# Moving small loads to ScalarE's queue and reordering the first chunk of a decayed attention with mixture-of-experts

## The chip, the cores and the metric

The kernel runs on one core of a Trainium2 chip. The metric is the device time of one execution in microseconds (us). Five engines work side by side on the core: TensorE (PE, matrix products and transposes), VectorE (DVE), ScalarE (ACT), GpSimd (POOL) and SyncE (SP, which here issues transfers between device memory and on-chip memory). Each engine takes its own instructions in order and waits on semaphores for the others. TensorE writes into PSUM, a small memory of a few named tiles, from which VectorE and ScalarE copy on.

## The reference

First a decayed linear attention over 4 sequences, 8 heads, 768 tokens and head size 48, all in float32:

```
state = alpha[t][:, None] * state + k[t] outer v[t]
y[t]  = q[t] @ state
```

Its output, 3072 tokens of 384 numbers, goes into a mixture of 8 experts with one expert chosen for each token:

```
logits = x @ w_gate + modality_bias[modality_id]
e      = argmax(logits);  gate = softmax(logits)[e]
out    = gate * (relu(x @ w1[e]) @ w2[e])
```

The inputs that the change touches are small: `w_gate` (384 x 8), `modality_bias` (2 x 8) and `modality_id` (3072 integers of 8 bytes, 24 KB).

## The kernel before, in words

**Attention.** The 3072 tokens are cut into 24 chunks of 128 tokens, six to a sequence. A loop over steps s = 0 to 23 works on several chunks at once, in the manner of a pipeline: in step s the decay of chunk s is made, chunk s-1 is scaled, scored and added to the state, chunk s-2 gives its outputs, and chunk s-3 goes to memory. For a chunk i:

- `decay_in` (L256) transposes alpha on TensorE (`trans`, L246) and copies it into the tile X, on VectorE for chunk 0 and on ScalarE for all others (L258).
- `decay` (L260) is a scan on VectorE that gives G, the products of the decays from a token to the end of the chunk (L263). `decay_back` (L268) takes a reciprocal and runs a second scan, Fw (L274), the other way.
- `scale` (L287) transposes the keys and multiplies them by G to give kh (L290), then transposes the queries and multiplies them by Fw to give qh (L293).
- `natural` (L296) transposes kh back, `scores` (L304) multiplies kh by qh, `state` (L325) and `outputs` (L335) make the outputs, `update` (L349) adds the chunk to the state.
- `rows` (L364) transposes the outputs of a chunk into rows and SyncE stores them (L374). `logits` and `logits_rows` (L376 to L391) multiply them by the gate weights `wgp`. `guard` (L277) is a check of alpha's range on ScalarE.

The tiles in PSUM that count here: "tr" has three buffers, taken in turn by all transposes of 128 x 512; "sc" has two, for the scores and small products of the routing; "kv" has one, shared by the state update, the logits and, in `bias_table` (L221), the transpose of the modality numbers.

**Loads.** Every chunk has four loads, of alpha, keys, queries and values, each 192 KB in rows of 192 bytes (`load`, L128). Thirteen of them are written ahead of the loop; in step s the loop adds alpha of chunk s+3 and the keys, queries and values of chunk s+2. Alpha, keys and queries have four buffers each, values six.

**The small loads.** `load_gate` (L152) fills `wgp` with four transfers of 3 KB in pieces of 32 bytes, called in step 1; GpSimd clears `wgp` first (L148). `load_modality` (L160) brings in `modality_id` (into `mi`) and `modality_bias` (into `mbb`), called in step 2. `mi` is first read in step 5 by `bias_table`, `wgp` in step 4 by `logits`. All are issued by SyncE.

**The zero matmuls.** `warm(n)` (L142) issues n products of a zero tile into a PSUM tile that nobody reads. Seven stand ahead of the loop, and `trans` adds one behind each of the transposes of chunks 0 and 1 and behind alpha of chunk 2.

**Order.** In the attention loop the instructions of TensorE, VectorE and ScalarE run in the order in which they are written. SyncE and GpSimd are ordered by a planner, which simulates the program with its own costs and may move an issue ahead of another that it takes to be held up. So SyncE's order isn't that of the text: what the profile shows behind the first thirteen loads is alpha 4, keys, queries and values 3, the gate loads, alpha 5, keys, queries and values 4, the modality loads, values 5, two stores of zeros, keys and queries 5, alpha 6.

**Experts.** From about 130 us on, tokens are routed to experts, gathered by index and put through the two layers, each float32 product split into three products of a faster type. TensorE is busy nearly without a break there.

Of the kernel before, what the change touches and what calls it, by code (L numbers as in the profile page):

```python
# [8 lines left out]
F32 = mybir.dt.float32  # L9
# [3 lines left out]
I32 = mybir.dt.int32  # L13
# [8 lines left out]
P = 128  # L22
B, H, S, D = 4, 8, 768, 48
# [5 lines left out]
E = 8  # L29
F = 1024  # L30
NM = 2
N = B * S
NU = N // P
# [29 lines left out]
def attention_moe(ctx: ExitStack, tc: tile.TileContext, q, k, v, alpha, mid, wg, mb, w1, w2, out):  # L63
    nc = tc.nc
    vec, act, pool, pe, sp = nc.vector, nc.scalar, nc.gpsimd, nc.tensor, nc.sync
# [9 lines left out]
    ps = ctx.enter_context(tc.tile_pool(name="ps", bufs=1, space=PSUM))  # L75
# [11 lines left out]
    for i in range(NB):  # L87
        for n, val in (("a", 1.0), ("k", 0.0), ("q", 0.0)):
            t = na.tile([P, H, 64], F32, name=f"nat_{n}{i}")
# [4 lines left out]
    for i in range(NV):  # L94
        t = ac.tile([P, H, 64], F32, name=f"vt{i}")
# [11 lines left out]
    st = {}  # L107
# [20 lines left out]
    def load(i, names="akqv"):  # L128
        b, c = divmod(i, NC)
        for n, t in (("a", alpha), ("k", k), ("q", q), ("v", v)):  # L130
            if n in names:
                dst = VT[i % NV][:, :, :D] if n == "v" else nat[n, i % NB][:, :, :D]
                sp.dma_start(dst, t[b, :, c * P : (c + 1) * P, :].rearrange("h t d -> t h d"))
# [8 lines left out]
    def warm(n):  # L142
        for _ in range(n):
            pe.matmul(idle, still[:, :P], still, start=True, stop=True)

    warm(7)
    wgp = ac.tile([P, 2, 2, 32], F32, name="wgp")
    pool.memset(wgp, 0.0)  # L148
    mi = ac.tile([NU, P, 2], I32, name="mi")
    mbb = ac.tile([P, NM, E], F32, name="mbb")  # L150

    def load_gate():  # L152
        for c in range(2):
            for g in range(2):
                sp.dma_start(
                    wgp[64 * c : 64 * c + D, g, :, :E],
                    wg.rearrange("(h c g d) e -> c g d h e", c=2, g=2, d=D)[c, g],
                )

    def load_modality():  # L160
        sp.dma_start(mi.rearrange("t p w -> t (p w)"), mid.bitcast(I32).rearrange("(t x) -> t x", t=NU))
        sp.dma_start(mbb, mb.unsqueeze(0).broadcast_to([P, NM, E]))


    DR = na.tile([P, SEGS], F32, name="DR")[:, : NP * SEG + 1]
    vec.memset(DR, 0.0)
    vec.memset(DR[:, SEG :: SEG], 1.0)
# [1 line left out]
    for i in range(2):  # L169
        t = na.tile([P, SEGS], F32, name=f"X{i}")[:, : NP * SEG + 1]  # L170
        vec.memset(t[:, 0 :: SEG], 0.0)
        X.append(t)
        t = na.tile([P, SEGS], F32, name=f"DF{i}")[:, : NP * SEG]
        vec.memset(t, 0.0)
        DF.append(t)
    for i in range(3):
        t = ac.tile([P, NP, 64], F32, name=f"T1{i}")
# [43 lines left out]
    def bias_table():  # L221
        mf = ac.tile([NU, P], F32, name="mf")
        vec.tensor_copy(mf, mi[:, :, 0])
        yield
        mp = ps.tile([P, NU], F32, name="kv")
        pe.transpose(mp, mf, ident[:NU, :NU])
        mt = ac.tile([P, NU], F32, name="mt")
        vec.tensor_copy(mt, mp)
        tmp = ac.tile([P, NU, E], F32, name="btt")
        for m in range(NM):  # L230
            sel = ac.tile([P, NU], F32, name=f"msel{m}")
            vec.tensor_scalar(sel, mt, float(m), None, op0=ALU.is_equal)
            vec.tensor_tensor(
                tmp if m else bt,
                sel.unsqueeze(2).broadcast_to([P, NU, E]),
                mbb[:, m].unsqueeze(1).broadcast_to([P, NU, E]),
                op=ALU.mult,
            )
            if m:
                vec.tensor_tensor(bt, bt, tmp, op=ALU.add)  # L240


    def seg(t, lo):
        return t.rearrange("p (a b) -> p a b", b=SEG)[:, :, lo : lo + P]

    def trans(i, n):  # L246
        p = ps.tile([P, NP, P], F32, name="tr", bufs=3)
        for j in range(NP):
            pe.transpose(
                p[:, j], nat[n, i % NB][:, 2 * j : 2 * j + 2].rearrange("p a b -> p (a b)"), ident  # L250
            )
        if i < 2 or (i == 2 and n == "a"):
            warm(1)
        return p

    def decay_in(i):  # L256
        pa = trans(i, "a")
        (act.copy if i else vec.tensor_copy)(seg(X[i % 2][:, 1:], 0), pa)  # L258

    def decay(i):  # L260
        x = X[i % 2]
        G = na.tile([P, SEGS], F32, name="G", bufs=4)[:, : NP * SEG + 1]
        vec.tensor_tensor_scan(  # L263
            G[:, 1:][:, ::-1], x[:, 1:][:, ::-1], DR[:, 1:][:, ::-1], 0.0, op0=ALU.mult, op1=ALU.add
        )
        st[i, "G"] = G

    def decay_back(i):  # L268
        x, d, G = X[i % 2], DF[i % 2], st[i, "G"]
        ac1 = amin[:, i]  # L270
        vec.tensor_scalar(ac1, G[:, 1::SEG], AFLOOR, None, op0=ALU.max)
        vec.reciprocal(d[:, 0::SEG], ac1)
        Fw = na.tile([P, SEGS], F32, name="Fw", bufs=3)[:, : NP * SEG]
        vec.tensor_tensor_scan(Fw, x[:, :-1], d, 0.0, op0=ALU.mult, op1=ALU.add)  # L274
        st[i, "F"] = Fw
# [8 lines left out]
            accum_out=gacc[:, i : i + 1],  # L284
        )

    def scale(i):  # L287
        kh = sb.tile([P, NP, P], F32, name="kh")
        pk = trans(i, "k")
        vec.tensor_tensor(kh, pk, seg(st[i, "G"][:, 1:], 1), op=ALU.mult)  # L290
        qh = sb.tile([P, NP, P], F32, name="qh", bufs=3)
        pq = trans(i, "q")
        vec.tensor_tensor(qh, pq, seg(st[i, "F"], 1), op=ALU.mult)  # L293
        st[i, "k"], st[i, "q"] = kh, qh

    def natural(i):  # L296
        p = ps.tile([P, NP, P], F32, name="tr", bufs=3)
        for j in range(NP):
            pe.transpose(p[:, j], st[i, "k"][:, j], ident)
        kn = na.tile([P, NP, P], F32, name="knat", bufs=2)  # L300
        act.copy(kn, p)
        st[i, "n"] = kn
# [61 lines left out]
    def rows(i):  # L364

        p = ps.tile([P, 2, NP, 64], F32, name="tr", bufs=3)
        for g in range(2):
            for h in range(2):
                pe.transpose(
                    p[:, g, 2 * h : 2 * h + 2].rearrange("p c e -> p (c e)"), st[i, "yt"][:, i % 2, g, h], ident  # L370
                )
        xs = sb.tile([P, DM], F32, name="xs", bufs=4)
        act.copy(xs.rearrange("p (j g d) -> p g j d", g=2, d=D), p[:, :, :, :D])
        sp.dma_start(xd[row(i) : row(i) + P, :], xs)  # L374
# [11 lines left out]
    def logits_rows(i):  # L386
        lp = ps.tile([P, 2, P], F32, name="kv")
        for c in range(2):
            pe.transpose(lp[:, c], st[i, "l"][:, c], ident)
        z = slice(i - 1, i + 1)  # L390
        vec.tensor_reduce(L[:, z], lp.rearrange("p c (j e) -> p c e j", e=32)[:, :, :E], axis=AX.X, op=ALU.add)  # L391
# [409 lines left out]
    def advance():  # L801
        for f in list(flows):
            if next(f, f) is f:
                flows.remove(f)

    def start(f):
        flows.append(f)
        if next(f, f) is f:
            flows.remove(f)
# [5 lines left out]
    def live(i):  # L815
        return 0 <= i < NU

    def groups(i):
        for after, t0, t1 in GROUPS:
            if after == i:  # L820
                start(group_flow(t0, t1))
# [28 lines left out]
    for s in range(NU):  # L850
        if s > 0 and s + PF < NU:
            load(s + PF, "a")
        if s > 0 and s + PF - 1 < NU:
            load(s + PF - 1, "kqv")
        if s == 1:
            load_gate()
        if s == 2:
            load_modality()
        if s == 4:
            sp.dma_start(xd[MID : MID + 1], zr)  # L860
            sp.dma_start(gd[MID : MID + 1], zr[:, 0:1])
        if s != 1:
            decay_in(s)
        if live(s - 1):
            scale(s - 1)
        if s == 1:
            decay_in(s)
        if live(s - 3):
            rows(s - 3)
        if live(s - 4) and s % 2:  # L870
            logits_rows(s - 4)
        advance()
        if live(s - 1) and (s - 1) % NC < NC - 1:
            natural(s - 1)
        decay(s)
        if s < NU - 1:
            advance()
        if s % 2:
            groups(s - 4)
        decay_back(s)  # L880
        guard(s)
        if s == 5:
            start(bias_table())
            half_index()
        if live(s - 3) and (s - 3) % 2:
            logits(s - 3)
        if live(s - 2):
            state(s - 2)
        if live(s - 1):
            scores(s - 1)  # L890
        if live(s - 2):
            outputs(s - 2)
        if live(s - 1):
            update(s - 1)

    L0 = NU - 1
    scale(L0)
    rows(L0 - 2)
    nctx.close()
# [65 lines left out]
    mp = ectx.enter_context(tc.tile_pool(name="mp", bufs=1, reuse_waits="tile"))  # L965
# [163 lines left out]
    for n in range(1, len(seq)):  # L1129
        kind, e = seq[n]  # L1130
# [4 lines left out]
        x, w = n % NX, n % 2  # L1135
# [117 lines left out]
```

## Time and profile before

| | |
|---|---|
| median of 3 runs | 374.81 us (373.77 to 374.91) |
| profiled execution | 375.57 us |
| its span, first to last instruction | 373.6 us |
| TensorE busy | 359.1 us |
| VectorE, ScalarE, GpSimd busy | 224.8, 189.0, 151.6 us |
| attention loop, first to last alpha transpose | 4.2 to 135.8 us |
| transfers | 59.18 MB, mostly in pieces under 512 bytes |

In the rows of a profile the first number is the start in us from the first instruction of the span and the second the duration. Then come the engine (PEld is TensorE's loading of weights, SPq SyncE's queue), the line of the kernel, the operation, output and inputs by tile name, and the shape. In brackets stands how long the engine was idle before, and whose end released it. `xN` says how many instructions of a kind a row merges. For an issue of a transfer the duration is that of the issue, not of the transfer. Rows of stretches give, for a stretch of time, the busy time and number of instructions of PE, PEld, DVE, ACT and POOL, the clock that TensorE was granted (1 is full), the mean load of the 16 DMA engines, and GB/s.

### The profile page before, as it was taken

Reading aid. Unit: us, or ns where it says so; the run is one execution under the profiler, and the core shown is the slowest. Engines: PE = TensorE matmul, PEld = TensorE weight load, DVE = VectorE, ACT = ScalarE, POOL = GpSimd, SP = SyncE. Lnnn points to the kernel's source line nnn. Section 1 sums busy time; section 2 is a strip of 40 time slices with the busy share of each in tenths; the row PEclk is TensorE's granted clock in tenths of the full one; section 3 lists DMA queues with packets and bytes.
Section 4 is the critical chain, followed back from the end, with each engine's and each line's share of the span. In section 5 each row is a group of like instructions: output and inputs, shape, how many; then the busy total and the mean of one; then the engine's idle time right before and its main releaser. Section 6 shows DMA issues by size and latency. Waiting matters only on the chain. (4 is left out here: it accounts for less than half of the span.)

```text
span 373.6 us, 9370 instructions
## 1 busy us (share of the span) xinstructions
PE 359.1 (96%) x3666; PEld 317.0 (85%) x3666; DVE 224.8 (60%) x455; ACT 189.0 (51%) x367; POOL 151.6 (41%) x218
## 2 busy tenths in 40 slices
PE   7998999999999899999999999999999999999992
PEld 4787788889888788799998898899889988978992
DVE  6886979878979977895746506531661455036400
ACT  2666677677678464446554425433551454154310
POOL 9945244534444345283146335412722372220021
PEclk9999999999999989999999999999999999999997
DMA  9989999999999994849756416431723374110011
GB/s 139 165 123 159 208 192 194 183 185 190 198 183 186 194 380 160 294 171 359 223 157 204 155 44 227 154 107 48 270 84 120 131 214 145 45 44 5 1 45 49
DMA packets 122846, 59.18 MB, mean 158 GB/s; under 512 B 102977, under 2 KB 114296, under 8 KB 122792
## 3 DMA queue, kind: packets, MB, share of 16 engines
q1 hardware_dynamic: 118824, 48.83, 58.5%
q0 software_dynamic: 3968, 9.65, 7.7%
q8 instruction: 31, 0.51, 0.6%
q14 instruction: 23, 0.19, 0.2%
HBM read 49.01 MB, written 9.50 MB: 157 GB/s over the span
## 5 line engine op out<-in xcount | busy, mean ns | idle before, releaser
L973 POOL DMA_INDIRECT out_dram<-os,odx x23 | 23.1, 1004 | 110.0 <-ACT os L1041 93.3
L1007 PE MATMUL sc<-w2H,hH 128*128 128x384 f32 x192 | 65.0, 338 | 0.0
L316 POOL TENSOR_SCALAR_AFFINE_SELECT scT<-scT 128x512 f32<-128x512 f32 x48 | 38.4, 822 | 65.3 <-ACT scT L315 65.3
L1009 PE MATMUL sc<-w2H,hL 128*128 128x384 f32 x192 | 64.2, 334 | 0.0
L1008 PE MATMUL sc<-w2L,hH 128*128 128x384 f32 x192 | 64.2, 334 | 0.0
L837 DVE TENSOR_TENSOR w1L<-w1r,w1H 128x768 fp32r<-128x768 f32 x24 | 22.0, 955 | 67.6 <-ACT w1H L835 67.6
L1026 PE MATMUL tr<-xH,w1H 128*128 128x512 f32 (+1 forms) x144 | 53.8, 374 | 0.0
L1028 PE MATMUL tr<-xH,w1L 128*128 128x512 f32 (+1 forms) x144 | 53.5, 372 | 0.0
L1027 PE MATMUL tr<-xL,w1H 128*128 128x512 f32 (+1 forms) x144 | 53.5, 371 | 0.0
L829 DVE SCALAR_TENSOR_TENSOR hL<-tr,hH 128x512 fp32r<-128x512 f32 x47 | 32.4, 689 | 31.5 <-ACT hH L827 31.3
L827 ACT ACTIVATE hH<-tr 128x512 fp32r<-128x512 f32 x47 | 28.1, 598 | 45.5 <-PE tr L1028 42.0
L1041 ACT ACTIVATE os<-sc,gg 128x384 f32<-128x384 f32 x23 | 13.4, 582 | 67.4 <-PE sc L1009 43.5
L1007 PEld LDWEIGHTS sc<-w2H,hH 128*128 128x128 f32 x192 | 36.1, 188 | 1.1 <-issue 1.0
L1008 PEld LDWEIGHTS sc<-w2L,hH 128*128 128x128 f32 x192 | 36.1, 188 | 0.0
L1009 PEld LDWEIGHTS sc<-w2H,hL 128*128 128x128 f32 x192 | 36.0, 188 | 0.0
L699 POOL DMA_INDIRECT gg<-gd,idx x25 | 26.6, 1063 | 21.9 <-DMA gd<-gs 14.9
L315 ACT COPY scT<-sc 128x512 f32<-128x512 f32 x48 | 25.8, 589 | 12.6 <-PE sc L311 12.6
L693 POOL DMA_INDIRECT xg<-xd,idx x25 | 27.0, 1081 | 11.7 <-issue 4.9
L274 DVE TENSOR_TENSOR_SCAN Fw<-X,DF 128x516 f32<-128x516 f32 x24 | 31.0, 1291 | 0.8
L1028 PEld LDWEIGHTS tr<-xH,w1L 128*128 128x128 f32 x144 | 27.1, 188 | 4.7
L1026 PEld LDWEIGHTS tr<-xH,w1H 128*128 128x128 f32 x144 | 27.1, 188 | 4.6
L1027 PEld LDWEIGHTS tr<-xL,w1H 128*128 128x128 f32 x144 | 27.1, 188 | 4.6
(245 smaller groups left out, 684.2 us busy)
## 6 DMA issues: line engine op xcount, KB each, us to landing
w1r<-in_moe_w_dram SPq DMA_DIRECT2D x16, 768.0 KB, 4.8
w2r<-in_moe_w_dram SPq DMA_DIRECT2D x16, 768.0 KB, 4.5
nat_a<-in_alpha_dram SPq DMA_DIRECT2D x24, 192.0 KB, 3.7
nat_k<-in_k_dram SPq DMA_DIRECT2D x24, 192.0 KB, 5.5
nat_q<-in_q_dram SPq DMA_DIRECT2D x24, 192.0 KB, 4.8
vt<-in_v_dram SPq DMA_DIRECT2D x24, 192.0 KB, 4.6
xd<-xs SPq DMA_DIRECT2D x24, 192.0 KB, 4.9
xg<-xd,idx POOLq DMA_INDIRECT x25, 5.4
```

The source lines that it names most:

```text
L274: vec.tensor_tensor_scan(Fw, x[:, :-1], d, 0.0, op0=ALU.mult, op1=ALU.add)
L316: pool.affine_select(s, s, [[0, NP], [1, P]], ALU.is_ge, 0.0, base=0, channel_multiplier=-1)
L693: pool.indirect_dma_start(xg[x][:, u], None, xd[0:rows], IOA(idx[:, c : c + 1], 0), bounds_check=rows - 1, oob_is_err=False)
L699: pool.indirect_dma_start(gg[x][:, u : u + 1], None, gd[0:rows], IOA(idx[:, c : c + 1], 0), bounds_check=rows - 1, oob_is_err=False)
L827: act.activation(hH, hp, AF.Relu)
L829: vec.scalar_tensor_tensor(hL, hp, 0.0, hH.bitcast(F32), op0=ALU.max, op1=ALU.subtract)
L1007: pe.matmul(op, hH[:, us] if f is None else hH[:, f, us], wH, start=first, stop=False)
L1008: pe.matmul(op, hH[:, us] if f is None else hH[:, f, us], wL, start=False, stop=False)
L1009: pe.matmul(op, hL[:, us] if f is None else hL[:, f, us], wH, start=False, stop=final)
L1026: pe.matmul(hp, wH[:, d, fs], XH[:, d, :n], start=(d == 0), stop=False)
L1027: pe.matmul(hp, wH[:, d, fs], XL[:, d, :n], start=False, stop=False)
L1028: pe.matmul(hp, wL[:, d, fs], XH[:, d, :n], start=False, stop=(d == ND - 1))
```

## The change

Five edits. ScalarE issues the four gate loads, ahead of the loop, and the modality and bias loads, at the top of step 3 ahead of that step's alpha copy; SyncE issues none of them any more. `wgp` is cleared on VectorE instead of GpSimd. The transpose of the modality numbers goes into "sc" instead of "kv". A zero matmul stands behind the transposes of chunk 0 and behind alpha of chunk 1 only. For chunk 0 the keys are transposed and scaled in step 0, between the two scans, by a new function `scale_keys`; for all other chunks `scale` calls it, with the same order as before.

```diff
-    pool.memset(wgp, 0.0)
+    vec.memset(wgp, 0.0)
     mi = ac.tile([NU, P, 2], I32, name="mi")
     mbb = ac.tile([P, NM, E], F32, name="mbb")
 
-    def load_gate():
-        for c in range(2):
-            for g in range(2):
-                sp.dma_start(
-                    wgp[64 * c : 64 * c + D, g, :, :E],
-                    wg.rearrange("(h c g d) e -> c g d h e", c=2, g=2, d=D)[c, g],
-                )
-
-    def load_modality():
-        sp.dma_start(mi.rearrange("t p w -> t (p w)"), mid.bitcast(I32).rearrange("(t x) -> t x", t=NU))
-        sp.dma_start(mbb, mb.unsqueeze(0).broadcast_to([P, NM, E]))
-
-
+    for c in range(2):
+        for g in range(2):
+            act.dma_start(
+                wgp[64 * c : 64 * c + D, g, :, :E],
+                wg.rearrange("(h c g d) e -> c g d h e", c=2, g=2, d=D)[c, g],
+            )
...
-        mp = ps.tile([P, NU], F32, name="kv")
+        mp = ps.tile([P, NU], F32, name="sc", bufs=2)
...
-        if i < 2 or (i == 2 and n == "a"):
+        if i == 0 or (i == 1 and n == "a"):
             warm(1)
...
-    def scale(i):
+    def scale_keys(i):
         kh = sb.tile([P, NP, P], F32, name="kh")
         pk = trans(i, "k")
         vec.tensor_tensor(kh, pk, seg(st[i, "G"][:, 1:], 1), op=ALU.mult)
+        st[i, "k"] = kh
+
+    def scale(i):
+        if i:
+            scale_keys(i)
         qh = sb.tile([P, NP, P], F32, name="qh", bufs=3)
         pq = trans(i, "q")
         vec.tensor_tensor(qh, pq, seg(st[i, "F"], 1), op=ALU.mult)
-        st[i, "k"], st[i, "q"] = kh, qh
+        st[i, "q"] = qh
...
-        if s == 1:
-            load_gate()
-        if s == 2:
-            load_modality()
         if s == 4:
             sp.dma_start(xd[MID : MID + 1], zr)
             sp.dma_start(gd[MID : MID + 1], zr[:, 0:1])
+        if s == 3:
+            act.dma_start(mi.rearrange("t p w -> t (p w)"), mid.bitcast(I32).rearrange("(t x) -> t x", t=NU))
+            act.dma_start(mbb, mb.unsqueeze(0).broadcast_to([P, NM, E]))
...
         decay(s)
+        if s == 0:
+            scale_keys(s)
```

## The prediction

> **What bounds the kernel now.** I read the shares of the page first, then the list of who waited for whom on TensorE, then the timeline around the one wait that ends on a transfer, then SyncE's queue ahead of it. Of the page:
>
> ```profile
> PE 359.1 (96%) x3666; PEld 317.0 (85%) x3666; DVE 224.8 (60%) x455; ACT 189.0 (51%) x367; POOL 151.6 (41%) x218
> ```
>
> TensorE is the bound, so what changes the end is TensorE's idle time, or work taken off it. The waits of its matmuls, total, times and longest:
>
> ```profile
> PE tr L249 <- DMA nat_a<-in_alpha_dram: 1.8, 1, 1.8
> ...
> PE kv L381 <- DVE mt L228: 0.4, 1, 0.4
> ```
>
> Both touch the change. The timeline shows them in steps 5 to 7 of the attention loop (start, duration, engine, line; in brackets the idle time ahead and what ended it):
>
> ```profile
> 33.01 1.23 DVE L274 TENSOR_TENSOR_SCAN Fw<-X,DF 128x516 f32<-128x516 f32 x1
> ...
> 33.84 0.62 PE L356 MATMUL kv<-vt,knat 128*64 128x48 f32 x16
> ...
> 34.16 0.59 DVE L223 CAST mf<-mi 24x128 f32<-24x128 int32 x1
> ...
> 35.88 0.17 DVE L523 TENSOR_REDUCE sz<-hz 128x1 f32<-128x13 f32 x1
> 36.24 0.42 PEld L249 LDWEIGHTS tr<-ident,nat_a 128*128 128x128 f32 x4 [1.91 <-DMA nat_a<-in_alpha_dram]
> 36.24 0.66 PE L249 MATMUL tr<-ident,nat_a 128*128 128x128 f32 x4 [1.78 <-DMA nat_a<-in_alpha_dram]
> ...
> 37.38 0.69 DVE L290 TENSOR_TENSOR kh<-tr,G 128x512 f32<-128x512 f32 x1 [1.33 <-PE tr L249]
> ...
> 38.81 0.64 PE L381 MATMUL kv<-yt,wgp 128*32 128x256 f32 x8 [0.41 <-DVE mt L228]
> ...
> 43.33 0.66 DVE L290 TENSOR_TENSOR kh<-tr,G 128x512 f32<-128x512 f32 x1
> ...
> 44.04 0.65 PE L299 MATMUL tr<-ident,kh 128*128 128x128 f32 x4
> ```
>
> TensorE is ready for step 6 at 33.84 + 0.62 = 34.46 and gets alpha chunk 6 only at 36.24: 1.78 us lost. VectorE loses less. Its scan of step 5 and the four small instructions behind it (34.16 to 36.05) run during the wait, and its key scaling at 37.38 is 1.33 late. From there VectorE works on without a gap until the next key scaling ends at 43.99, and TensorE's key transposes at 44.04 start on that. So in these steps VectorE is late next: however early chunk 6 lands, at most 1.33 us come back.
>
> Why is the chunk late? SyncE's issues ahead of it:
>
> ```profile
> 16.87 1.97 SPq L133 DMA_DIRECT2D nat_q<-in_q_dram  x1
> 18.89 1.12 SPq L133 DMA_DIRECT2D vt<-in_v_dram  x1
> 20.11 3.58 SPq L155 DMA_DIRECT2D wgp<-in_moe_w_gate_dram  x4
> 23.79 0.38 SPq L133 DMA_DIRECT2D nat_a<-in_alpha_dram  x1
> ...
> 26.41 1.37 SPq L161 DMA_DIRECT2D mi<-in_moe_modality_id_dram  x1
> 27.82 0.36 SPq L162 DMA_DIRECT2D mbb<-n_moe_modality_bias_dram  x1
> ...
> 28.75 0.39 SPq L860 DMA_DIRECT2D xd<-zr  x1
> ...
> 31.27 1.07 SPq L133 DMA_DIRECT2D nat_a<-in_alpha_dram  x1
> ```
>
> SyncE issues back to back, about 1.1 us a load while the DMA engines are full. Chunk 6 is issued at 31.27 and is there at 36.24, 4.97 later. The four gate loads, 12 KB in all, hold the queue for 3.58 us, and the DMA engines run dry behind them (last two numbers: DMA share, GB/s):
>
> ```profile
> 22.00:23.00 1.00, 1.00 (x27) 0.95 (x24) 0.81 (x1) 1.00 (x3) 0.75 (x1) 1.00 0.24 23
> 23.00:24.00 1.00, 1.00 (x10) 1.00 (x11) 0.00 (x0) 0.80 (x3) 1.00 (x3) 1.00 0.12 9
> ```
>
> **The change part by part.** *SyncE loses six issues.* Behind the v load, which ends at 20.01, stand seven loads, two small stores and then chunk 6. At 1.12 and a gap of 0.06 a load, and 0.45 a store, chunk 6 is issued at 20.06 + 7 × 1.18 + 0.9 = 29.2 and lands at 29.2 + 4.97 = 34.2. VectorE needs the step's key transposes by 36.05, and these end 37.38 − 36.24 = 1.14 after the step starts, so 34.9 is early enough. The margin of 0.7 is less than one issue: if the planner, which orders SyncE anew, puts one more load ahead, about 0.5 of the gain is lost; two cost all of it. Gain: −1.33.
>
> *Zero matmuls.* Three of seven go, all of them in step 2. The rows of the first steps:
>
> ```profile
> 4.12 1.28 ACT L278 ACT_TABLE_LOAD   x1 [4.12 <-DMA nat_a<-in_alpha_dram]
> ...
> 8.45 0.58 ACT L258 COPY X<-tr 128x512 f32<-128x512 f32 x1 [2.32 <-PE tr L249]
> ...
> 9.21 0.67 DVE L290 TENSOR_TENSOR kh<-tr,G 128x512 f32<-128x512 f32 x1
> ...
> 9.80 0.68 DVE L293 TENSOR_TENSOR qh<-tr,Fw 128x512 f32<-128x512 f32 x1
> ...
> 10.03 0.63 PE L299 MATMUL tr<-ident,kh 128*128 128x128 f32 x4 [1.40 <-DVE kh L290]
> 10.39 1.22 DVE L263 TENSOR_TENSOR_SCAN G<-X,DR 128x516 f32<-128x516 f32 x1
> ...
> 10.58 1.10 PE L311 MATMUL sc<-qh,kh 48*64 48x128 f32 x32
> ...
> 12.71 0.38 PE L144 MATMUL y<-still 128*128 128x512 bf16 x1
> ...
> 12.93 0.60 PE L249 MATMUL tr<-ident,nat_k 128*128 128x128 f32 x4
> ...
> 13.57 0.69 DVE L290 TENSOR_TENSOR kh<-tr,G 128x512 f32<-128x512 f32 x1 [0.27 <-PE tr L249]
> ```
>
> Without the zero matmul at 12.71 the key transposes start in its place, 0.22 earlier, and VectorE's scaling at 13.57, idle for 0.27 on them, moves with them: −0.22. The other two stand between transposes that then wait for VectorE anyway: nothing. Could TensorE's clock fall instead? The granted clock (third number from the end) stayed at 1.00 through the idle stretches of 1.40 ahead of 10.03 and 1.78 ahead of 36.24, and the zero matmuls that go stand amid dense work:
>
> ```profile
> 10.00:11.00 1.00, 0.97 (x20) 0.83 (x24) 1.00 (x2) 0.31 (x1) 0.92 (x2) 1.00 1.50 164
> ...
> 36.00:37.00 1.00, 0.76 (x7) 0.76 (x8) 0.05 (x1) 0.06 (x1) 0.41 (x1) 1.00 0.72 121
> ```
>
> No cost, then. The Trainium skill (TensorE: Matmul & The Clock Gate, HAM oscillation) warns that an idle gap of more than about 3.4 us halves the clock; by that rule too nothing happens here, unless gaps add up.
>
> *Keys of chunk 0 ahead of its second scan.* VectorE is busy without a gap over these rows, so the query scaling at 9.80 ends at the same time in either order, and the scores at 10.58 start on it. Only the key transposes at 10.03 come earlier, into TensorE's idle time. Zero; the bound on the gain is that idle time, 1.40, and a cost would need chunk 0's key load later than the scan's end.
>
> *The modality transpose in another PSUM tile.* The 0.41 ahead of 38.81 goes, but VectorE sets 37.38 to 43.99, so it becomes slack: zero (bounds −0.41 and 0). *Clearing the gate tile on VectorE*: it is idle before the first alpha copy; zero.
>
> *Gate loads on ScalarE at the start.* ScalarE waits for chunk 0 until 4.12, and its next copy that others need is at 8.45, idle for 2.32 before: four issues at the 0.36 to 0.9 that such small ones take on SyncE (27.82; 3.58/4) fit. Their packets go beside chunk 0's load, which everything follows. From below 0; from above, 12 KB as four of SyncE's issues, 3.58. The nearest row is 27.82's 0.36 for one small transfer in flight before chunk 0 is complete, shared with it; I take +0.1.
>
> *Modality and bias loads on ScalarE in step 3.* They stand in ScalarE's own order, ahead of the alpha copy (X) of step 3:
>
> ```profile
> 17.62 0.33 ACT L358 COPY S<-kv 128x192 f32<-128x192 f32 x1
> ...
> 18.17 0.59 ACT L258 COPY X<-tr 128x512 f32<-128x512 f32 x1 [0.22 <-PE tr L249]
> ...
> 18.84 0.62 PE L369 MATMUL tr<-ident,yt 128*128 128x128 f32 x4
> ...
> 19.35 0.66 PE L299 MATMUL tr<-ident,kh 128*128 128x128 f32 x4
> ```
>
> Behind the waiting issue stands that copy, and behind the copy stand the output transposes at 18.84: with three buffers named tr they take over the alpha transposes' buffer, and 18.84 is the copy's end, 18.76, and a hop. TensorE has no slack from here to step 6. No row shows an issue on ScalarE. From below: two at 27.82's 0.36 with gaps of 0.05, begun when the copy to S has been dispatched at 17.62, end at 18.44, 0.27 after 18.17; the key transposes at 19.35 can take 0.07 of it: +0.2. (An issue that costs ScalarE nothing: 0.) From above: SyncE's own 1.37 + 0.36 + 0.1 end at 19.45, +1.2. I take +0.2, as SyncE's 1.37 was behind four queued loads and ScalarE's queue is empty then.
>
> **Sum**: −1.33 − 0.22 + 0.1 + 0.2 = −1.25. The profiled execution took 375.57 (span 373.6, 1.97 around it), which gives 374.32; it lies 0.76 above the median of the runs shown, 374.81. On that median the forecast is 373.56, say 373.6. Its own range is 372.9 to 374.6: with the 0.41 ahead of 38.81 and chunk 0 on time, or with SyncE's 1.2 for ScalarE.
>
> **Rivals.** *ScalarE's issues queue behind SyncE's.* While SyncE issues without a pause (16.87 to 23.7), one of its issues takes 1.1 to 1.97. If an issue on ScalarE can only begin where one of SyncE's ends, the two of step 3 cost half a wait (0.57) + 0.36, then a full wait (1.14) + 0.36, with gaps 2.6. Begun 0.22 earlier than 17.62, they end at 20.0, and the X copy is 1.8 late. TensorE stands still ahead of 18.84 for as long. Then −1.33 + 1.8 + 0.1 = +0.6: 375.4, slower than before; with SyncE's longest issue in the way +2.0, 376.8. It decides from about 2 us for the two issues, where the loss equals the gain. For it: SyncE's issue times follow the load on the DMA engines, 0.38 when they are dry and 1.1 when full, so an issue does wait for something shared. Against it: ScalarE has no load of its own outstanding then. The Trainium skill (Perfetto Trace Analysis, DMA Instruction — HWDGE) says that the two issuing sequencers share one descriptor generator, locked for the length of an issue; by that rule this rival holds, and the time is its 375.4. No row here shows two sequencers issuing at once.
>
> *Chunk 6 lands no earlier.* The DMA engines are full, or the planner fills the freed places with loads and stores that were further back. Then −0.22 + 0.3 remain: 374.8. For it: only 0.7 of margin. Against it: the two windows in which the engines are dry, over 2 us of transfer time.
>
> *The gate loads delay chunk 0.* If its load lands with or after the four, everything behind 4.12 shifts by up to 3.58, the stall's end included, since VectorE's chain sets that. It decides at 1.3 us; at 2.5 the sum is −1.33 + 2.5, 376.0. Against it: chunk 0 is issued first and 16 times as large as the four together.
>
> **How the numbers follow.** 0.3% of the time is 1.12 us, about what a measurement of this kernel tells from none. Forecast 0.52 (faster 0.38, same 0.14: its −1.25 is near the bound). Queueing on ScalarE 0.26 (faster 0.02, same 0.15, slower 0.09). Chunk 6 no earlier 0.12 (same 0.11, slower 0.01). Late chunk 0 0.10 (same 0.04, slower 0.06). Together faster 0.40, same 0.44, slower 0.16. TensorE's clock adds spread that the change doesn't steer: it dropped once,
>
> ```profile
> 130.00:135.00 5.00, 5.00 (x80) 3.69 (x79) 4.79 (x20) 2.25 (x6) 2.38 (x3) 0.66 1.03 388
> ```
>
> and a third of the clock for 5 us is 1.7 us, which may be there or not. The range 372.7 to 375.9 leaves out the upper parts of the two slow rivals (0.11) and a run without that drop on top of the full gain (0.07).
>
> **What would show it.** In the changed kernel TensorE should list no wait on an alpha load, and VectorE's first key scaling after its four small instructions should follow them with no idle time; the key transposes of step 7 should wait about 0.9 on VectorE. The X copy of step 3 should start 0.1 to 0.4 after its transposes plus the usual 0.2 idle; 1.5 or more means queueing. ScalarE's four issues at the start should take under 1 us each, and its table load should start at 4.1 to 4.3. Wrong it would be if the wait on chunk 6 stays, if the output transposes of step 3 wait on X for over a microsecond, or if a later wait of the same size takes over.

## The result: 3.1% slower

The changed kernel takes 386.48 us in the median (385.74 to 388.01), the kernel before 374.86 beside it; the ratio is 1.031, with a 95% interval of 1.025 to 1.036. The forecast was 373.6, and the time lies 10.6 us above the upper end of its range. The profiled execution took 386.31, its span is 384.2 against 373.6. The ratios in this document leave out the few executions that ran at a lower clock and more than 1.5% longer than the fastest of their kernel.

The list of waits of the changed kernel has a new head on TensorE and a new entry on ScalarE (total, times, longest):

```profile
PE tr L367 <- ACT X L251: 12.6, 1, 12.6
```

and on ScalarE:

```profile
ACT X L251 <- DMA vt<-in_v_dram: 13.0, 1, 13.0
```

One wait of 12.6 us, once, is longer than the whole loss of 11.6. TensorE waits for ScalarE's alpha copy X, and ScalarE waits for a load of *values*, which its copy doesn't read. The wait on alpha chunk 6, 1.78 before, is gone from TensorE's list. The timeline of the changed kernel around the stall, ScalarE first, then SyncE, then TensorE:

```profile
17.49 0.32 ACT L356 COPY S<-kv 128x192 f32<-128x192 f32 x1
29.12 0.56 ACTq L857 DMA_DIRECT2D mi<-in_moe_modality_id_dram  x1
30.34 0.36 ACTq L858 DMA_DIRECT2D mbb<-n_moe_modality_bias_dram  x1
30.80 0.59 ACT L251 COPY X<-tr 128x512 f32<-128x512 f32 x1 [12.98 <-DMA vt<-in_v_dram]
...
23.86 2.29 SPq L133 DMA_DIRECT2D vt<-in_v_dram  x2
...
28.61 1.07 SPq L133 DMA_DIRECT2D nat_a<-in_alpha_dram  x1
29.77 1.27 SPq L133 DMA_DIRECT2D vt<-in_v_dram  x1
...
17.34 0.66 PE L242 MATMUL tr<-ident,nat_a 128*128 128x128 f32 x4
...
18.27 0.60 PE L242 MATMUL tr<-ident,nat_q 128*128 128x128 f32 x4
31.43 1.12 PE L367 MATMUL tr<-ident,yt 128*128 128x128 f32 x4 [12.56 <-ACT X L251]
...
37.87 0.66 PE L242 MATMUL tr<-ident,nat_a 128*128 128x128 f32 x4
...
43.85 0.66 PE L242 MATMUL tr<-ident,nat_a 128*128 128x128 f32 x4
...
57.68 0.66 PE L297 MATMUL tr<-ident,kh 128*128 128x128 f32 x4 [0.95 <-DVE kh L283]
...
61.22 0.66 PE L242 MATMUL tr<-ident,nat_a 128*128 128x128 f32 x4
...
147.59 0.66 PE L242 MATMUL tr<-ident,nat_a 128*128 128x128 f32 x4
```

The alpha transposes in it (nat_a) begin steps 3, 4, 5, 8 and 23. Those of the kernel before, steps 4, 5, 8 and 23:

```profile
22.89 0.66 PE L249 MATMUL tr<-ident,nat_a 128*128 128x128 f32 x4
...
28.87 0.66 PE L249 MATMUL tr<-ident,nat_a 128*128 128x128 f32 x4
...
47.57 0.66 PE L249 MATMUL tr<-ident,nat_a 128*128 128x128 f32 x4
...
135.50 0.66 PE L249 MATMUL tr<-ident,nat_a 128*128 128x128 f32 x4
```

The issues themselves are short, 0.56 and 0.36, close to the two at 0.36 of the forecast. What it didn't have is the time ahead of them: ScalarE has nothing to do after 17.81 and issues the modality ids only at 29.12.

The stall costs more than its own length. The stretches of the changed kernel (last three numbers: granted clock, DMA share, GB/s):

```profile
22.00:23.00 1.00, 0.00 (x0) 0.00 (x0) 0.00 (x0) 0.00 (x0) 0.00 (x0) 1.00 0.93 174
23.00:24.00 1.00, 0.00 (x0) 0.00 (x0) 0.00 (x0) 0.00 (x0) 0.00 (x0) 0.55 1.00 171
31.00:36.00 5.00, 4.57 (x56) 4.01 (x56) 2.81 (x4) 2.05 (x5) 0.00 (x0) 0.50 1.11 176
130.00:135.00 5.00, 5.00 (x94) 4.18 (x93) 4.84 (x15) 4.21 (x10) 2.03 (x3) 1.00 0.60 130
```

TensorE's clock falls about 4 us after the last matmul (18.87) and is still at half when the work resumes. From the output transposes of step 3 to the next alpha transposes it takes 37.87 − 31.43 = 6.44 us, against 22.89 − 18.84 = 4.05 in the kernel before: 2.39 more. The Trainium skill (TensorE: Matmul & The Clock Gate, HAM oscillation) puts the limit for such a gap at about 3.4 us; for this gap the trace agrees.

The account by the starts of the steps: step 4 begins 14.98 later than before (12.59 of stall and 2.39 of slow clock), step 5 too, step 8 13.65 later. So 1.33 us come back between steps 5 and 8. The drop of the clock between 130 and 135 us (0.66 before) isn't there: the row above has 1.00, and in the trace's clock record it stays at 1.00 from 36.7 to 381.5 us. Step 23 stands at +12.09, 1.56 less than step 8. That is about what the drop costs, half of the 3.4 us from 130.1 to 133.5 in the kernel before. The spans differ by 10.6. What makes the 1.5 us between 12.09 and 10.6, in the experts' part, stays open.

### The profile page after: what moved, and what is told of

It reads as the page before. It is cut to its first block, busy times and chain, and to the rows that moved or that the text cites. A ratio compares the mean times of both kernels' runs of the same rounds, so it can differ in the third digit from the quotient of the medians.

```text
span 384.2 us, 9361 instructions
## 1 busy us (share of the span) xinstructions
PE 358.8 (93%) x3663; PEld 317.4 (83%) x3663; DVE 225.1 (59%) x456; ACT 189.3 (49%) x367; POOL 151.2 (39%) x217
## 5 line engine op out<-in xcount | busy, mean ns | idle before, releaser
L314 POOL TENSOR_SCALAR_AFFINE_SELECT scT<-scT 128x512 f32<-128x512 f32 x48 | 37.6, 807 | 77.5 <-ACT scT L313 77.5
L256 DVE TENSOR_TENSOR_SCAN G<-X,DR 128x516 f32<-128x516 f32 x24 | 29.6, 1232 | 11.7 <-ACT X L251 11.7
L691 POOL DMA_INDIRECT xg<-xd,idx x25 | 27.0, 1079 | 11.6 <-issue 5.2
```

Source lines behind the costliest of these rows:

```text
L256: vec.tensor_tensor_scan(G[:, 1:][:, ::-1], x[:, 1:][:, ::-1], DR[:, 1:][:, ::-1], 0.0, op0=ALU.mult, op1=ALU.add)
L314: pool.affine_select(s, s, [[0, NP], [1, P]], ALU.is_ge, 0.0, base=0, channel_multiplier=-1)
L691: pool.indirect_dma_start(xg[x][:, u], None, xd[0:rows], IOA(idx[:, c : c + 1], 0), bounds_check=rows - 1, oob_is_err=False)
```

## The experiments

**Theory and rivals.** The program as built (a listing of its instructions, no profile) shows what ScalarE waits for. Every transfer of SyncE and ScalarE reports its end on one of eight counters. The counters are handed out in turn, in the order of the planner, and an issue waits until the last transfer on its counter, eight places earlier, is complete:

```
place  engine   transfer       counter  waits for
24     SyncE    values 4       0        place 16
25     SyncE    values 5       1        place 17
26-31  SyncE    zeros, zeros, keys 5, queries 5, alpha 6, values 6
32     ScalarE  modality ids   0        place 24
33     ScalarE  bias           1        place 25
```

In the kernel before, SyncE holds all of these places and comes to them in order, so such a wait looks eight of its own transfers back. ScalarE reaches its two places at 17.8 us, as nothing else holds it; SyncE reaches place 24 at 23.86 and place 25 at 25.00. That is theory A.

The trace of the changed kernel bears the listing out. Its records name the counter (a semaphore) on which each transfer reports and the one for which each issue waits. The modality ids wait for the counter of values 4, whose last report comes at 29.10, and are issued at 29.12. The bias waits for that of values 5, whose last report comes at 30.32, and is issued at 30.34.

The rivals: theory B is the forecast's first rival, ScalarE's issues queueing behind SyncE's for a generator of descriptors; theory C, that another part of the change makes the stall.

**1. The two loads back on SyncE.**

```diff
+        if s == 2:
+            sp.dma_start(mi...); sp.dma_start(mbb...)
-        if s == 3:
-            act.dma_start(mi...); act.dma_start(mbb...)
```

> The change, with only the two loads of step 3 (modality ids, bias) given back to SyncE in step 2. Theory A (each transfer of SyncE and ScalarE takes the next of eight completion counters in the order of the written program, and its issue waits for the transfer eight places earlier; the two loads in step 3 fall behind the transfers of values 4 and 5, which SyncE issues only at 23.9 and 25.0 us): no wait of ScalarE before its copy of step 3, 373.4 us (372.6 to 374.4). Theory B (issues of ScalarE queue behind those of SyncE in one generator): the same here, 373.4, as ScalarE issues nothing in the loop. Theory C (some other part of the change makes the stall, the two loads only stand beside it): the stall of 12.6 us stays, 386.

Measured: 375.85 beside 377.15 for the kernel before on the same chip, ratio 0.996 (0.9941 to 0.9979). No long wait on ScalarE or TensorE. C falls: the other parts of the change together are a gain of 0.4%.

**2. The same two loads, ScalarE, step 1.**

```diff
-        if s == 3:
+        if s == 1:
             act.dma_start(mi...); act.dma_start(mbb...)
```

> The change, with the same two loads issued by ScalarE in step 1 in place of step 3, about 8 us after the start and in the midst of SyncE's first twenty issues. Theory A: eight places earlier stand gate loads 1 and 2, done by 6 us: no wait of ScalarE, 373.3 us (372.5 to 374.4). Theory B: SyncE issues without a gap from 5 to 20 us, so ScalarE's two issues wait for several of its issues of 1.1 us each, or for all of them: 376 to 386 us. Theory C: 386.

Measured: 0.997 (0.9953 to 0.9988). ScalarE's rows of this kernel:

```profile
4.36 0.56 ACTq L857 DMA_DIRECT2D mi<-in_moe_modality_id_dram  x1
5.49 0.36 ACTq L858 DMA_DIRECT2D mbb<-n_moe_modality_bias_dram  x1
```

The issues have the same durations as in the slow kernel, while SyncE issues its first loads beside them. This speaks against B. The expectation put them about 8 us after the start; in fact ScalarE came to them right behind the gate loads. The second was held even here, but briefly: it waits for the second gate load, whose last report comes at 5.47, and is issued at 5.49.

**3. The kernel before with these two loads alone moved to ScalarE's step 3.**

> The kernel before, with only the two loads moved from SyncE's step 2 to ScalarE's step 3; gate loads stay on SyncE. Theory A: the two wait for the transfers of values 4 and 5, which SyncE, behind its gate loads, issues later than in the changed kernel (25.6 and about 27 us in place of 23.9 and 25.0), so ScalarE's copy of step 3 starts at 32 to 33 us in place of 30.8: 386 to 389 us. Theory B: two waits of one issue each, up to 3.6 us: 376 to 378. Theory C: 374 to 375.

Measured: ratio 1.034 (1.031 to 1.037). ScalarE and SyncE in this kernel:

```profile
29.41 0.61 ACTq L861 DMA_DIRECT2D mi<-in_moe_modality_id_dram  x1
30.60 0.36 ACTq L862 DMA_DIRECT2D mbb<-n_moe_modality_bias_dram  x1
31.07 0.59 ACT L258 COPY X<-tr 128x512 f32<-128x512 f32 x1 [13.61 <-DMA vt<-in_v_dram]
...
24.32 2.14 SPq L133 DMA_DIRECT2D vt<-in_v_dram  x2
```

The two loads by themselves make the whole loss. The copy starts at 31.07, earlier than the 32 to 33 expected: the expectation took the issue of values 4 from the kernel before (25.6), but here SyncE spent 2.52 us on the four gate loads, not 3.58, and was there at 24.32.

**4 and 5. ScalarE in step 2, and in step 4.** As in experiment 2, with other steps. If A holds, the wait isn't tied to step 3 but to whatever stands eight places ahead: queries 3 and alpha 5 for step 2, queries 5 and alpha 6 for step 4.

> The change, with the same two loads issued by ScalarE in step 2. Theory A: eight places earlier stand the transfers of queries 3 (issued by SyncE at 18.2 us) and of alpha 5 (at 20.5), which land some 5 us after their issue; ScalarE comes to the loads at about 13 us and is held until about 25: a stall of 11 to 12 us, now in step 2, 384 to 387 us. Theory B: the same place in SyncE's row of issues as step 1 has, so a time as in that run, 376 to 386. Theory C: the stall stays in step 3, 386.

> The change with the two loads issued by ScalarE in step 4 in place of step 3. Theory A (counters): eight places earlier stand the transfers of queries 5 and of alpha chunk 6, issued by SyncE at about 28 to 30 us and there some 5 us later; ScalarE comes to the loads at about 23 and is held until 33 to 35, now ahead of its alpha copy of step 4: TensorE stands still for 10 to 11 us ahead of the output transposes of step 4, its clock falls to 0.5, and the ratio is 1.025 to 1.035. Theory B (the issue queues behind SyncE's open issues for a generator): SyncE's gaps grow from 26 us on, so the wait is shorter than in step 3, under 4 us, ratio 0.997 to 1.008.

Measured: 1.036 (1.0324 to 1.0396) in step 2 and 1.029 (1.0258 to 1.033) in step 4. SyncE's and ScalarE's rows, first of the kernel with step 2:

```profile
18.32 1.00 SPq L133 DMA_DIRECT2D nat_q<-in_q_dram  x1
...
20.24 1.16 SPq L133 DMA_DIRECT2D nat_a<-in_alpha_dram  x1
...
23.10 0.56 ACTq L857 DMA_DIRECT2D mi<-in_moe_modality_id_dram  x1
25.50 0.36 ACTq L858 DMA_DIRECT2D mbb<-n_moe_modality_bias_dram  x1
25.96 0.59 ACT L251 COPY X<-tr 128x512 f32<-128x512 f32 x1 [12.82 <-DMA mi<-in_moe_modality_id_dram]
```

then of the kernel with step 4:

```profile
27.61 0.86 SPq L133 DMA_DIRECT2D nat_q<-in_q_dram  x1
28.56 1.06 SPq L133 DMA_DIRECT2D nat_a<-in_alpha_dram  x1
...
32.69 0.56 ACTq L857 DMA_DIRECT2D mi<-in_moe_modality_id_dram  x1
33.89 0.36 ACTq L858 DMA_DIRECT2D mbb<-n_moe_modality_bias_dram  x1
34.35 0.58 ACT L251 COPY X<-tr 128x512 f32<-128x512 f32 x1 [11.11 <-DMA nat_a<-in_alpha_dram]
```

From the issue of the transfer eight places ahead to ScalarE's issue, in us:

| loads in | first load | second load |
|---|---|---|
| step 2 | queries 3: 23.10 − 18.32 = 4.78 | alpha 5: 25.50 − 20.24 = 5.26 |
| step 3 (the change) | values 4: 29.12 − 23.86 = 5.26 | values 5: 30.34 − 25.00 = 5.34 |
| step 3 (alone) | values 4: 29.41 − 24.32 = 5.09 | values 5: 30.60 − 25.25 = 5.35 |
| step 4 | queries 5: 32.69 − 27.61 = 5.08 | alpha 6: 33.89 − 28.56 = 5.33 |

The issue times 25.00 and 25.25 are those of the second issue in merged rows of two, from the trace's own records. Eight times nearly the same gap, and it is what such a transfer takes from issue to landing in the changed kernel between 14 and 45 us (KB each, median us to landing):

```profile
vt<-in_v_dram SPq DMA_DIRECT2D x7, 192.0 KB, 5.0
...
nat_a<-in_alpha_dram SPq DMA_DIRECT2D x5, 192.0 KB, 5.1
nat_q<-in_q_dram SPq DMA_DIRECT2D x5, 192.0 KB, 5.2
```

This is A, to the transfer. In all eight cases the trace names the counter of the transfer in the table as the one that the issue waits for, and its last report comes 0.02 us before the issue: in step 2 at 23.08 and 25.48, in step 4 at 32.67 and 33.87. No rival is left for the stall. Step 2's ratio, 388 us on the 374.86 of before, is a little above the 384 to 387 us expected and step 4's TensorE wait, 9.6 us, a little under the 10 to 11.

**6. The two loads issued by GpSimd.** In the listing, and in the trace, GpSimd's transfers have counters of their own.

```diff
-            act.dma_start(mi...); act.dma_start(mbb...)
+            pool.dma_start(mi...); pool.dma_start(mbb...)
```

> The change with the two loads of step 3 issued by GpSimd in place of ScalarE. Theory A: in the written program GpSimd's transfers have completion counters of their own, so nothing waits for values 4 and 5 and the stall is gone: ratio 0.995 to 0.998; if GpSimd's issues hold up its first selections (TensorE's step 1 begins after 8.3 us), 0.998 to 1.002. Theory C (the two loads hold up the loop by being in flight in step 3): the stall stays, 1.03.

Measured: 0.9991 (0.9968 to 1.0014), no stall; GpSimd issued the two at 5.41 and 6.16 us without a wait. The engine that issues and the counters change together here, so by itself it doesn't tell A from B; the interval spans both of A's bands.

**7. The gate loads alone on ScalarE.** The kernel before, with `wgp` cleared on VectorE and its four loads issued ahead of the loop by ScalarE.

> The kernel before, with only the four gate loads moved from SyncE to ScalarE ahead of the loop (and the gate tile cleared on VectorE, as this needs). Theory A (the prediction's step 1, with four issues in place of six): SyncE is ahead by 1.0 us or more when it comes to alpha chunk 6, TensorE's wait of 1.78 on it falls to at most 0.3, and VectorE's chain lets 1.3 come back; the gate issues cost 0.05 us at the start: ratio 0.9965 (0.9945 to 0.9985). Theory B (the gain needs the other parts): ratio 1.000.

Measured: 0.9973 (0.9951 to 0.9996). A holds: TensorE no longer waits on alpha chunk 6, and step 8 begins at 46.47, 1.10 earlier than before. As far as these intervals can tell, this part by itself brings all that the change can bring.

**8 and 9. The zero matmuls.** First the kernel before without the three zero matmuls; then the kernel of experiment 2 with all seven again.

> The kernel before, with only the three zero matmuls of step 2 left out. Theory A (the prediction's step 2): step 3 begins 0.1 to 0.2 us earlier, TensorE's clock stays at 1.00 between 10 and 20 us, and the wait on alpha chunk 6 eats the gain: ratio 0.999 to 1.000. Theory B (these matmuls held the clock up): the clock falls to 0.5 for some 3.3 us in step 2, as it did where the two loads stood in step 1 (0.71, 0.50, 0.50, 0.58 from 12 to 16 us), step 3 begins 1.0 to 1.2 later, and the same wait eats that too, down to 0.7: ratio 1.000 to 1.003. The rows of 12 to 18 us tell the two apart, not the time.

> The change with the two loads issued by ScalarE in step 1, as before, and with the seven zero matmuls of the kernel before. Theory B (the zero matmuls hold the clock): the clock stays at 1.00 from 12 to 16 us, step 3 begins at 17.4 to 17.6 us in place of 18.53, and the time falls by up to 1.1 us against that run, to a ratio of 0.994 to 0.996 against the kernel before. Theory A (the drop there had another cause): the drop stays, ratio 0.997 to 0.998.

The reason for asking is in experiment 2's kernel, whose clock fell at the start:

```profile
12.00:13.00 1.00, 1.00 (x18) 0.95 (x15) 0.93 (x3) 1.00 (x3) 1.00 (x5) 0.71 1.41 162
13.00:14.00 1.00, 1.00 (x6) 1.00 (x5) 0.56 (x1) 0.71 (x2) 1.00 (x2) 0.50 1.43 162
...
15.00:16.00 1.00, 0.98 (x5) 0.72 (x4) 0.86 (x2) 0.00 (x0) 0.23 (x1) 0.58 1.46 168
```

and on TensorE's timeline:

```profile
10.69 1.10 PE L309 MATMUL sc<-qh,kh 48*64 48x128 f32 x32 [1.45 <-DVE qh L291]
...
18.53 0.66 PE L242 MATMUL tr<-ident,nat_a 128*128 128x128 f32 x4
```

Its step 3 starts at 18.53, the changed kernel's at 17.34. With the seven zero matmuls (experiment 9) the clock is at 1.00 there and step 3 starts at 17.55. But the time doesn't follow: 0.9971 (0.9952 to 0.9989), as with four. The kernel before without three of them measured 1.0035 (1.0002 to 1.0068). Its profiled execution, 375.25 us, has the clock at 1.00 from 12 to 17 us and step 3 at 17.25, 0.23 earlier than before, as the forecast had it. The mean clock of its executions was 0.991 in the median, against 0.994 for the kernel before. 0.3% of the clock is about the size of the loss; where in those executions it falls isn't shown, and the other kernels with four zero matmuls and no stall have medians of 0.992 to 0.993, where the kernel before has 0.992 to 0.994. So: 0.2 us earlier in the rows, no gain in the time, and a clock that may fall. More isn't settled.

**10. The key scaling alone.**

> The kernel before, with only chunk 0's key scaling moved ahead of its second scan. The prediction's step 3: key transposes of chunk 0 about 1.4 us earlier, its scores within 0.1 of 10.58 us, ratio 0.999 to 1.001. Rival (in the runs with this part the scores began at 10.66 to 10.69 us, in the run with the gate loads alone at 10.16): the key scaling stands in VectorE's row ahead of the second scan and the query scaling ends 0.1 later, which the wait on alpha chunk 6 eats: ratio 1.000 to 1.001 with scores at 10.65 to 10.75.

Measured: 1.0026 (1.0002 to 1.0051). VectorE and TensorE in this kernel:

```profile
8.73 1.23 DVE L274 TENSOR_TENSOR_SCAN Fw<-X,DF 128x516 f32<-128x516 f32 x1
10.06 0.69 DVE L298 TENSOR_TENSOR qh<-tr,Fw 128x512 f32<-128x512 f32 x1
...
10.81 1.10 PE L316 MATMUL sc<-qh,kh 48*64 48x128 f32 x32 [1.70 <-DVE qh L298]
```

The scores begin 0.23 later than the 10.58 of before, a little beyond the rival's 10.75. In the kernel before the key scaling stands between the second scan and the query scaling and starts at 9.21, 0.08 ahead of the scan's end in the profile (8.06 + 1.23 = 9.29). Here the query scaling follows directly on the scan that it reads, and starts 0.10 after its end (9.96). In these rows an instruction that reads the result of the one just before it pays for that, and an independent one in between hides it. The cost is there in every kernel: from the end of the first scan to the query scaling it takes 2.18 to 2.32 us in the five kernels with the old order and 2.46 to 2.55 in the nine with the new one.

The wait on alpha chunk 6 didn't take this up, as the rival had it, since that chunk came 0.22 later too (step 6 at 36.46 in place of 36.24). Step 8 even begins 0.80 later than before (48.37). The rest of that arises between 39 and 43 us, in two small instructions of VectorE: one starts after 0.33 us of idle time, another takes 0.64 in place of 0.17. The kernel of experiment 7, which leaves the key scaling where it was, has the same two, so they can't be laid to this edit; what makes them stays open. So of the 0.26% measured here, about 1 us, only some 0.2 are shown to be the key scaling's.

**11 and 12. The two loads ahead of the loop on ScalarE**, first with the rest of the change, then with only the early loads and the modality transpose in "sc" (seven zero matmuls, the key scaling where it was).

> The change with the two loads issued by ScalarE ahead of the loop, with the gate loads. By the counters the later of the two waits only for the first gate load, done by 6 us: no wait of ScalarE in the loop, SyncE six issues lighter, alpha chunk 6 there before TensorE asks: ratio 0.995 to 0.9965. If the clock falls in step 2 as in the run with the loads in step 1, 1.1 us of it goes: 0.998. If six small loads at the start hold up chunk 0 (table load of ScalarE after 4.6 us): 0.998 to 1.002.

> The kernel before, with the gate loads and the two loads of step 2 issued by ScalarE ahead of the loop, the gate tile cleared on VectorE, and the modality transpose in the scores' tile; zero matmuls and the order of the key scaling stay as before. Scores of chunk 0 at 10.2 to 10.6 us, no drop of the clock between 10 and 20 us, no wait over 0.3 us on alpha chunk 6: ratio 0.994 to 0.997, not worse than any kernel so far. If the zero matmuls and the key scaling were a gain: 0.997 to 0.999.

Measured: 0.9971 (0.9953 to 0.9989) and 0.9967 (0.9938 to 0.9995). Both beat the kernel before, and the changed kernel by far. Experiments 1, 2, 7, 9, 11 and 12, at 0.996 to 0.997, can't be told apart.

## Why the prediction was wrong

**Modality and bias loads on ScalarE in step 3: the step that failed.** It took "two at 27.82's 0.36 with gaps of 0.05, begun when the copy to S has been dispatched at 17.62". The durations were nearly right (0.56 and 0.36). The begin wasn't, 29.12 in place of 17.62, nor was the gap, 0.66 in place of 0.05. The forecast named what stands behind the issue, the X copy and the output transposes, and that TensorE has no slack there; but it treated the issue as free to begin when ScalarE comes to it, and priced only its length, in the upper bound of +1.2 too. It carries a wait for the transfer eight places earlier in the planner's order. The cost was 12.59 + 2.39 = 14.98 us in place of 0.2. Of the signs of being wrong that the prediction named, one came: the output transposes of step 3 waited on X for far more than a microsecond.

**Queueing behind SyncE**, the rival at 375.4, named the right place and the wrong mechanism. ScalarE's 0.56 for the modality ids, 29.12 to 29.68, lies wholly inside SyncE's alpha issue of 28.61 to 29.68. Its 0.36 for the bias, 30.34 to 30.70, lies wholly inside SyncE's values issue of 29.77 to 31.04, and is what the same load took on SyncE in the kernel before (27.82). So here an issue on one engine doesn't wait until the other engine's has ended. The Trainium skill (Perfetto Trace Analysis, DMA Instruction — HWDGE) says that the shared generator is locked for exclusive use until all descriptors of an issue have been generated; if that lock was at work here, it was held for less than an issue's row, and these two loads show no price for it.

**SyncE loses six issues: right.** Alpha chunk 6 was issued at 28.61 (forecast 29.2). The gain of 1.33 between steps 5 and 8 is there in the kernels of experiments 1, 2, 6, 9 and 11, to within 0.01. In those of 12 and 7 it is 1.04 and 0.82, where VectorE has the delays told in experiment 10, one of them or both. Steps 5 and 8 in the kernel of experiment 1:

```profile
28.75 0.66 PE L242 MATMUL tr<-ident,nat_a 128*128 128x128 f32 x4
...
46.12 0.66 PE L242 MATMUL tr<-ident,nat_a 128*128 128x128 f32 x4
```

The 47.57 − 28.87 = 18.70 us of the kernel before have become 46.12 − 28.75 = 17.37, which is −1.33; in the changed kernel it is 61.22 − 43.85 = 17.37 too. VectorE is late next as told. In experiment 9:

```profile
35.96 0.17 DVE L521 TENSOR_REDUCE sz<-hz 128x1 f32<-128x13 f32 x1
36.05 0.68 DVE L283 TENSOR_TENSOR kh<-tr,G 128x512 f32<-128x512 f32 x1
```

The key scaling follows the four small instructions with no idle time, and in the changed kernel the key transposes of step 7 wait 0.95 on VectorE (the row at 57.68), where about 0.9 was forecast.

**Gate loads at the start: right.** VectorE's first alpha copy moved from 5.32 to 5.37 in the changed kernel, +0.05 for the +0.1 taken. The kernel before, then the changed one:

```profile
5.32 0.69 DVE L258 COPY X<-tr 128x512 f32<-128x512 f32 x1 [2.42 <-PE tr L249]
...
1.37 3.08 ACTq L154 DMA_DIRECT2D wgp<-in_moe_w_gate_dram  x4
...
5.37 0.69 DVE L251 COPY X<-tr 128x512 f32<-128x512 f32 x1 [2.34 <-PE tr L242]
```

The same kind of wait is at work here, unpriced and harmless. Of the 3.08 us of the merged row the first three issues take until 2.73; the fourth waits for the counter of alpha chunk 0, whose last report comes at 4.11, and is issued at 4.13. ScalarE needs that chunk next in any case. Its table load starts at 4.48, where the prediction had 4.1 to 4.3.

**Modality transpose in "sc": right**; the wait of 0.41 is gone and nothing came of it.

**Zero matmuls: half right.** The 0.22 is there in the rows (0.23). "No cost, then" for the clock was too sure: it fell to 0.50 at 13 us in one kernel without any idle stretch longer than 1.45 us between the start of its work at full clock (5.6 us) and the fall, and the removal alone measured a little slower, not faster (1.0035, 1.0002 to 1.0068).

**Keys of chunk 0: wrong by 0.2 to 0.3 us.** The step said that "the query scaling at 9.80 ends at the same time in either order". It starts 0.26 later (10.06), since each scaling now stands right behind the scan that it reads.

Without the failed step and its +0.2 the sum is −1.45 us, on 374.8 a ratio of 0.9961. Experiment 1, where that step is undone, measured 0.996 (0.9941 to 0.9979), and its step 8 begins 47.57 − 46.12 = 1.45 earlier. Some of that agreement is luck: the gain of 0.22 and the loss of about 0.2 at chunk 0's keys cancel nearly, and SyncE still issues two of the six loads there. What carries the sum is the 1.33.

## What to carry to other kernels

A transfer moved to another engine's queue takes along waits that the source doesn't show. Read them from the built program, and ask of each issue which earlier transfer it waits for, which engine issues that one, and whether that engine is as far along in real time as in the planner's order. On an engine that also computes in order, put a load where that partner is long done (here ahead of the loop: 0.997) and not beside the backlog of another queue (1.03).

## What the runs showed that was not expected

- Two engines' issues run side by side (the bias load takes 0.36 us inside an issue of SyncE and 0.36 without one), while a shared set of completion counters held one of them for 11 us.
- A stall of 12.6 us on TensorE costs 2.4 us more after its end, since the clock stays at 0.50 for some 5 us of work (31.43 to 36.7).
- The clock can also fall amid work: to 0.50 between 12.4 and 15.8 us after idle stretches of at most 1.45 us, in one kernel and not in others with nearly the same rows. The Trainium skill (TensorE: Matmul & The Clock Gate, HAM oscillation) ties a fall to an idle gap of more than about 3.4 us; for this one no row shows such a gap, and its cause stays open.
- In the clock records each stretch at 0.50 within the work lasts 3.4 us or close to a multiple of it: 3.4 in experiment 2 and in the kernel before (130.1 to 133.5), 10.2 with the loads in step 4, 13.6 in the changed kernel, 17.1 in experiment 3. So a stall costs the slow clock up to the end of such a stretch, not only up to its own end.
